# Moving k's and q's transfers up, delaying a piece's rounding by two half iterations, and letting conversion steps into lighter slots of a one-core attention and two-layer MLP kernel

## The chip, the cores and the metric

The kernel runs on one core of a Trainium2 chip. The metric is the device time of one execution in microseconds, as a median over runs. The engines are named as in the profile: PE is the matrix engine (PEld its weight load), DVE, ACT and POOL are the vector, scalar and GpSimd engines, and SP is the queue that issues the transfers.

## The reference

For 8 batches of 8 heads with 576 positions of 64 values, 32 packed queries `p` attend to `k`, `v`; then `q` attends to the 32 results. The attention output, laid out as 4608 tokens of 512 values, goes through two layers:

```python
h = x @ w_in;  g = max(h, 0) + alpha * min(h, 0);  x = g @ w_out          # d_ff 2048
g = x @ w_gate;  y = (silu(g) * (x @ w_val)) @ w_out2                     # d_ff 1536
```

[...] Every weight is widened on the chip from its two 32-bit words to a 32-bit float, and then split into a rounded high part and a low part, so that three matmuls (low by high, high by high, high by low) give the product.

## The kernel before

**Two stages.** The first stage has 256 iterations `it` of the first layer. `h_unit(it)` makes 128 hidden values of half a batch (288 tokens), and `o_unit(it - 3)` multiplies those of three iterations ago by `w_out` into four PSUM accumulators (`LAG1 = 3`). The hidden PSUM tiles, `g32` and `m` have two buffers each. 32 iterations belong to a batch. The second stage has 72 steps of the second layer, `gv_step`, fed from DRAM copies of its split weights (`wgvd`, `wo2d`).

**Half iterations.** `plan` holds side work for each half iteration, called a slot (`slot = 2 * it + late`), so a batch has 64 slots. While the 64 slots of one batch run, `attention(b)` makes the next batch's attention, for b = 2 to 7, by the table `STEPS`: a number is the slot's offset in the 64, the names behind it are the steps. `k0` to `k3` and `q0` to `q3` are loads of two heads each, four DMAs a load. `kt0` to `kt3` and `qt0` to `qt3` transpose them on DVE (L620). `s1a`, `s1b` are the first logits on PE and need all four kt. `mx`, `exp`, `sums` are their softmax, `et0`, `et1` transposes of it on PE, `pp0`, `pp1` products with v, whose results ACT scales into `ppbd` (L708), `ppt` a transpose of `ppbd`. `s2a`, `s2b`, `top`, `sub`, `sum`, `mul`, `turn`, `rest` are the second attention.

**Weight conversion.** From slot 84 on, each slot ends with `more_weights2`, which advances a generator over the 36 pieces of the second layer's weights. A piece is fetched by one DMA (L931), then `widen` makes an absolute value on ACT (L224), five DVE steps (L226, L230, L239, L248, L256) and a sum on POOL (L267). `split2` then rounds a half of it on ACT (L943), takes the difference on POOL (L944) and stores both (L945). For w_gate and w_val there are differences of quarters on POOL (L961) as well, which are split too. The generator yields a letter ahead of each step: `v` for a DVE step, `p` for POOL and for a `split2`, `a` for the absolute value. A slot grants at most two v, two p and one a; a slot in the set `busy` (a step on DVE that is not in `LIGHT`, a `PPW` slot, a `LEAVE` slot) grants no v. The absolute value waits until `LANDING` slots after the slot of the fetch.

**What orders instructions.** Matmuls are in program order (`behind`). On DVE and ACT a slot's steps stand behind the previous iteration's `m` (L1033) and `g` (L1036), and the rounding `hi` (L1044) of two iterations ago. A planner orders the rest by program order and by when it expects operands, buffers and engines to be free. SP and POOL are tied by that alone. Tiles of the tag `u` (k, q, their transposes, E, ET, s2, a) share 8 buffers, which are given out in program order, so a load cannot be placed ahead of the buffers that the program asks for before it. Each engine then runs its own list in order.

Of the kernel before, what the change touches and what calls it, by code (L numbers as in the profile page):

```python
# [71 lines left out]


STEPS = """
    8:p,k0,k1 10:pt 11:kt0,k2 12:kt1,k3,v0 14:kt2 15:kt3 17:s1a 19:s1b 20:mx0,q0,q1 21:mx1,exp0
    22:exp1 23:sums 24:et0 26:pp0,v1 27:et1 28:qt0,q2 29:qt1,q3 33:qt2 34:qt3 35:pp1 37:ppt 40:s2a
    42:s2b 44:top0 45:top1 46:sub0 47:sub1 49:sum0 50:sum1 51:mul0 52:mul1 53:turn0 54:turn1
    57:rest0 58:rest1
"""

LIGHT = {"p", "pt", "et0", "et1", "pp0", "pp1", "ppt", "s1a", "s1b", "exp1", "sums"}
PPW = (48, 55, 60, 66)

LEAVE = (6, 7, 38, 39)
# [3 lines left out]


GROUP0 = 84  # L90
LANDING = 5


FIRST_X = dict(load=-36, A11=-27, S=-26, S2=-25, A12=-12, D4=-11, S3=-11, S1=-10, A22=-8, S4=-7)
# [11 lines left out]
def f32(ap):  # L106
    return ap.bitcast(F32)
# [3 lines left out]
def tile_kernel(  # L111
# [93 lines left out]
    def like(ap, other):  # L205

        return ap if len(other.shape) == 2 else ap.rearrange("p (c f) -> p c f", c=KC)
# [8 lines left out]
    def widen(src, raw, val, out=None, n_piece=-1):  # L216

        if src is not None:
            issued.append(nc.sync.dma_start(out=like(raw, src), in_=src))
        words = raw.rearrange("p (n t) -> p n t", t=2)  # L220
        low, high = words[:, :, 0], words[:, :, 1]
        held = n_piece in HOLD
        with tc.issue_after(begun[HOLD[n_piece]].ins) if held else ExitStack():
            nc.scalar.activation(out=f32(val), in_=f32(high), func=AF.Abs)  # L224
        yield "v"
        nc.vector.tensor_scalar(  # L226
            out=f32(val), in0=f32(val), scalar1=E_TOP, scalar2=E_LOW, op0=ALU.min, op1=ALU.max
        )
        yield "v"
        nc.vector.tensor_scalar(  # L230
            out=val,
            in0=val,
            scalar1=3,
            scalar2=0x3FFFFFF8,
            op0=ALU.logical_shift_left,
            op1=ALU.bitwise_and,
        )
        yield "v"
        nc.vector.scalar_tensor_tensor(  # L239
            out=val,  # L240
            in0=high,
            scalar=0xC0000000,
            in1=val,
            op0=ALU.bitwise_and,
            op1=ALU.bitwise_or,
        )
        yield "v"
        nc.vector.tensor_scalar(  # L248
            out=high, in0=val, scalar1=0xFF800000, scalar2=None, op0=ALU.bitwise_and
        )  # L250
        yield "v"
        if n_piece in BY_POOL:
            nc.scalar.activation(out=f32(low), in_=low, func=AF.Copy, scale=2.0**-52)
            nc.gpsimd.tensor_tensor(out=f32(low), in0=f32(low), in1=f32(high), op=ALU.mult)
        else:
            nc.vector.scalar_tensor_tensor(  # L256
                out=f32(low),
                in0=low,
                scalar=2.0**-52,
                in1=f32(high),  # L260
                op0=ALU.mult,
                op1=ALU.mult,
            )
        yield "p"
        full = f32(val) if out is None else like(f32(val), out)
        other = f32(low) if out is None else like(f32(low), out)
        nc.gpsimd.tensor_tensor(  # L267
            out=full if out is None else out, in0=full, in1=other, op=ALU.add
        )
# [542 lines left out]
    for f in range(NF1):  # L812
# [8 lines left out]
        a=quad(0),  # L821
        b=quad(1, ["h"], evac=nc.vector),
        c=quad(2),
        d=quad(3, ["h", "at"]),
# [47 lines left out]
    def at(it, late, fn):  # L872

        plan.setdefault((it, late), []).append(fn)
# [7 lines left out]
                order += [(j, f, f == fs[0], f == fs[-1]) for f in fs]  # L882

    NB1 = 2 * NF1
    busy = set()
    for key, script in EARLY.items():
        at(*key, lambda script=script: run(script))

    for b in range(2, B):
        d0 = 2 * NB1 * (b - 1)  # L890
        steps_of = attention(b)
        for entry in STEPS.split():
            d, names = entry.split(":")
            slot = d0 + int(d)
            for n in names.split(","):
                at(*divmod(slot, 2), steps_of[n])
                if n[1:].isdigit() or n in LIGHT:
                    continue
                busy.add(slot)
        for j, d in enumerate(PPW):  # L900
            at(*divmod(d0 + d, 2), lambda b=b, j=j: pp_win(b, j))
            busy.add(d0 + d)
        busy.update(d0 + d for d in LEAVE)

# [3 lines left out]
    spots = {}  # L910

    def weights2():
        a, b = (t for t in raw_tiles)
        spots["raw"] = a[:, :1024]
        spots["g"], spots["v"] = a[:, 1024:1536], a[:, 1536:2048]
        spots["st"] = [b[:, i * 512 : (i + 1) * 512] for i in range(4)]
        spots["n"] = 0
# [9 lines left out]
    def fetch2():  # L927

        src = next(coming, None)
        if src is not None:  # L930
            nc.sync.dma_start(out=like(spots["raw"], src), in_=src)  # L931
            spots["landed"] = spots["slot"] + LANDING

    def piece2(name):
        yield "a"
        yield from widen(None, spots["raw"], spots[name])

    def split2(full, out):

        stage = spots["st"][spots["n"] % 4].bitcast(F32R)  # L940
        spots["n"] += 1
        hi, lo = stage[:, :256], stage[:, 256:]
        nc.scalar.activation(out=hi, in_=full, func=AF.Copy)  # L943
        nc.gpsimd.tensor_tensor(out=lo, in0=full, in1=f32(hi), op=ALU.subtract)  # L944
        nc.sync.dma_start(out=out, in_=f32(stage).rearrange("p (t n) -> p t n", t=2))  # L945

    def all_weights2():


        weights2()  # L950
        gv = {n: f32(spots[n]) for n in "gv"}
        b11, b21 = gv["g"][:, :256], gv["g"][:, 256:]
        b12, b22 = gv["v"][:, :256], gv["v"][:, 256:]
        fetch2()
        for f in range(NF2):

            def split(k, full):
                split2(full, wgvd[f][:, :, k, :])

            def less(out, x, y):  # L960
                nc.gpsimd.tensor_tensor(out=out, in0=x, in1=y, op=ALU.subtract)  # L961

            yield from piece2("g")
            yield "p"
            fetch2()
            split(0, b11)
            yield "p"
            split(2, b21)
            yield from piece2("v")
            yield "p"  # L970
            fetch2()
            split(6, b22)
            for out, x, y in (b11, b12, b11), (b12, b22, b12), (b22, b22, b11), (b21, b21, b22):
                yield "p"
                less(out, x, y)
            for k, full in (4, b11), (3, b12), (1, b22), (5, b21):
                yield "p"
                split(k, full)
            yield from piece2("g")
            for t in range(2):  # L980
                yield "p"
                if t == 0:
                    fetch2()
                c = slice(256 * t, 256 * t + 256)
                split2(gv["g"][:, c], wo2d[f][:, :, c])

    work2 = all_weights2()
    kinds = []

    def more_weights2(vector, slot):  # L990

        spots["slot"] = slot
        left = dict(v=2 if vector else 0, p=2, a=1)
        if not kinds:
            kinds.append(next(work2, None))
        while kinds[0] is not None and left[kinds[0]]:
            if kinds[0] == "a" and slot < spots["landed"]:
                return
            left[kinds[0]] -= 1
            kinds[:] = [next(work2, None)]  # L1000
# [318 lines left out]
    def steps(it, late):  # L1319


        with ExitStack() as held:
            if chained:
                for ins in made.get(it - 1), begun.get(it - 1), rounded.get(it - 2):
                    if ins is not None:
                        held.enter_context(tc.issue_after(ins.ins))
            for s in plan.get((it, late), ()):
                s()
            slot = 2 * it + late
            if slot >= GROUP0:  # L1330
                more_weights2(slot not in busy, slot)

    due = []
    for it in range(N1 + LAG1):
        if it == CHAIN0:
            chained.append(it)
        steps(it, 0)
        if it < N1:
            h_unit(it)
        steps(it, 1)  # L1340
        due.extend(range(max(it - LAG1, 0), it - LAG1 + 1))

        if it < N1 and len(due) == 1 and order[due[0]][2]:
            continue
        while due:
            o_unit(due.pop(0))
# [44 lines left out]
```

## Time and profile before

| | |
|---|---|
| median of 3 runs | 1673.23 us (1671.7 to 1676.21) |
| the profiled execution | 1670.67 us, its span 1668.9 us |
| PE busy | 1602.7 us, 96% of the span |
| DVE, ACT, POOL busy | 52%, 41%, 42% |
| mean granted clock of PE | 0.982 of full speed |

The span runs from the first to the last instruction of the profiled execution. A busy share is a sum over stages with different limits; PE's ends of matmuls are modelled.

### The profile page before, as it was taken

What the parts mean: (1) busy time and instruction counts of PE and PEld (TensorE: products, weight loads), DVE (VectorE), ACT (ScalarE), POOL (GpSimd) and SP (SyncE); (2) the same over time, 40 slices, a digit from 0 to 9 for tenths busy, and PEclk for the clock granted to TensorE, in tenths of its full rate; (3) what the DMA queues carried; (4) which work ended last, traced back from release to release, by engine and by line L of the source; (5) the groups of instructions that cost most, each with busy time, mean ns of one, the idle gap of its engine ahead of it and who ended that gap; (6) DMA issues with size and microseconds to landing.
All of it is one profiled execution on the core that took longest, in us unless ns stands there. A gap on an engine that the chain in (4) does not pass through costs nothing.

```text
span 1668.9 us, 28555 instructions
## 1 busy us (share of the span) xinstructions
PE 1602.7 (96%) x10708; PEld 1451.7 (87%) x10708; DVE 873.4 (52%) x1549; ACT 678.6 (41%) x1523; POOL 706.5 (42%) x764
## 2 busy tenths in 40 slices
PE   5798899999999999999999999999999999999997
PEld 3567698888898989889999999999999999999997
DVE  6989757575666667575334433442442443344222
ACT  5765655555565555555422222232232222223222
POOL 3556754565565555656223222322322322232222
PEclk7799999999999999999999999999999999999999
DMA  9433464635646363652654563464455456445342
GB/s 235 128 106 108 124 159 126 168 113 140 167 118 181 99 176 95 158 162 88 231 202 157 187 217 139 180 228 148 177 179 206 166 181 215 147 163 208 141 175 82
DMA packets 230443, 266.12 MB, mean 159 GB/s; under 512 B 130464, under 2 KB 196000, under 8 KB 230304
## 3 DMA queue, kind: packets, MB, share of 16 engines
q1 hardware_dynamic: 230304, 264.30, 50.5%
q8 instruction: 84, 1.38, 0.4%
q14 instruction: 55, 0.45, 0.1%
HBM read 214.70 MB, written 49.55 MB: 158 GB/s over the span
## 4 chain that ended last, share of the span: by engine, by line
PE 55%; issue 18%; POOL 9%; DVE 9%; DMA 5%; ACT 2%; SPq 2%; POOLq 0%; DVEq 0%; ACTq 0%
PE acc L1059 5%; PE acc L1060 4%; PE acc L1065 4%; PE o L308 4%; PE o L309 4%; PE o L307 4%; POOL pl L1278 3%; PE yb L307 3%; PE yb L309 3%; PE yb L308 3%; PE h L307 2%; PE h L309 2%; PE h L308 2%; PE xb L308 2%; PE vb L308 2%
## 5 line engine op out<-in xcount | busy, mean ns | idle before, releaser
L1046 POOL TENSOR_TENSOR lo<-g,hi 128x288 fp32r<-128x288 f32 x256 | 228.0, 892 | 242.6 <-ACT hi L1044 194.1
L1258 POOL TENSOR_TENSOR s<-s,u 128x384 f32<-128x384 f32 x72 | 73.1, 1015 | 490.5 <-ACT s L1252 490.5
L1036 DVE SCALAR_TENSOR_TENSOR g<-h,sg,m 128x288 f32<-128x288 f32 x256 | 130.2, 509 | 170.4 <-ACT m L1033 146.3
L1215 DVE TENSOR_TENSOR u<-yb,p 128x384 f32<-128x384 f32 x144 | 80.1, 556 | 255.2 <-PE yb L309 255.2
L1278 POOL TENSOR_TENSOR pl<-s,ph 128x384 fp32r<-128x384 f32 x144 | 145.4, 1031 | 106.5 <-ACT ph L1276 104.7
L1215 DVE TENSOR_TENSOR u<-vb,u 128x384 f32<-128x384 f32 x144 | 80.4, 558 | 197.7 <-PE vb L309 197.6
L1044 ACT ACTIVATE hi<-g 128x288 fp32r<-128x288 f32 x256 | 112.8, 441 | 151.7 <-DVE g L1036 149.5
L307 PE MATMUL h<-a2h,ppw 128*128 128x288 f32 x512 | 160.4, 313 | 13.1 <-DVE g L1036 7.7
L309 PE MATMUL o<-wp,ph 128*128 128x512 f32 x432 | 171.4, 397 | 0.0
L308 PE MATMUL o<-wp,ph 128*128 128x512 f32 x432 | 170.9, 396 | 0.0
L307 PE MATMUL o<-wp,pl 128*128 128x512 f32 x432 | 168.8, 391 | 0.9 <-POOL pl L1278 0.9
L1252 ACT ACTIVATE s<-p 128x384 f32<-128x384 f32 x72 | 37.9, 526 | 302.0 <-DVE p L1215 302.0
L309 PE MATMUL h<-a2l,ppw 128*128 128x288 f32 x512 | 152.3, 297 | 0.0
L308 PE MATMUL h<-a2h,ppw 128*128 128x288 f32 x512 | 151.9, 297 | 0.0
L1033 ACT ACTIVATE m<-h,sal 128x288 f32<-128x288 f32 x256 | 126.0, 493 | 51.7 <-PE h L309 50.7
L307 PE MATMUL yb<-ring,gv 128*128 128x384 f32 x432 | 145.9, 338 | 0.4 <-DVE u L1215 0.3
L309 PE MATMUL yb<-ring,gv 128*128 128x384 f32 x432 | 144.4, 334 | 0.0
L308 PE MATMUL yb<-ring,gv 128*128 128x384 f32 x432 | 144.4, 334 | 0.0
L307 PEld LDWEIGHTS h<-a2h,ppw 128*128 128x128 f32 x512 | 97.4, 190 | 44.7 <-DVE g L1036 14.5
L1276 ACT ACTIVATE ph<-s 128x384 fp32r<-128x384 f32 x144 | 69.8, 519 | 121.3 <-DVE s L1256 121.2
L309 PEld LDWEIGHTS h<-a2l,ppw 128*128 128x128 f32 x512 | 97.2, 190 | 0.8 <-issue 0.8
L308 PE MATMUL vb<-ring,gv 128*128 128x384 f32 x288 | 97.6, 339 | 0.0
(228 smaller groups left out, 4178.3 us busy)
## 6 DMA issues: line engine op xcount, KB each, us to landing
gv<-wgvd SPq DMA_DIRECT2D x144, 896.0 KB, 5.7
wgvd<-cva SPq DMA_DIRECT2D x84, 256.0 KB, 3.1
cva<-in_moe_w_out_dram SPq DMA_DIRECT2D x28, 512.0 KB, 4.1
v<-in_v_dram SPq DMA_DIRECT2D x16, 576.0 KB, 5.6
out_dram<-os SPq DMA_DIRECT2D x12, 768.0 KB, 3.8
cva<-in_moe_w_in_dram SPq DMA_DIRECT2D x16, 512.0 KB, 3.9
kr<-in_k_dram SPq DMA_DIRECT2D x96, 72.0 KB, 2.9
qr<-in_q_dram SPq DMA_DIRECT2D x96, 72.0 KB, 2.6
```

The lines of the kernel that those rows point to most:

```text
L307: nc.tensor.matmul(o, wlo, xhi, start=start, stop=False, **kw)
L308: nc.tensor.matmul(o, whi, xhi, start=False, stop=False, **kw)
L309: return nc.tensor.matmul(o, whi, xlo, start=False, stop=stop, **kw)
L1033: begun[it] = nc.scalar.activation(out=m, in_=hp, func=AF.Copy, scale=sal[:, f : f + 1])
L1036: made[it] = nc.vector.scalar_tensor_tensor(out=g32, in0=hp, scalar=sg[:, f : f + 1], in1=m, op0=ALU.mult, op1=ALU.max)
L1044: rounded[n] = nc.scalar.activation(out=hi, in_=x, func=AF.Copy)
L1046: nc.gpsimd.tensor_tensor(out=lo, in0=x, in1=f32(hi), op=ALU.subtract)
L1059: nc.tensor.matmul(acc[dc], lo[:, f % WP, c], ghi, start=start, stop=False)
L1215: return nc.vector.tensor_tensor(out=out, in0=bank, in1=x, op=ALU.add)
L1258: latest.append(nc.gpsimd.tensor_tensor(out=s2, in0=s2, in1=u3, op=ALU.mult))
L1276: nc.scalar.activation(out=hi, in_=x, func=AF.Copy)
L1278: nc.gpsimd.tensor_tensor(out=lo, in0=x, in1=f32(hi), op=ALU.subtract)
```

## The change

`STEPS` gives k0, k1 at offset 2 and k2, k3 at 3, ahead of all transposes of k (before: 8, 8, 11, 12, with k2 and k3 behind kt0 and kt1). q0, q1 go from 20 to 17, q2 from 28 to 25, q3 stays at 29; p goes from 8 to 5. After a piece's sum, the generator fetches the next source at once and yields `w`, which holds it until `SETTLE = 2` slots after the slot of the sum, so that the first rounding comes then. Roundings have a letter of their own, `s`, one a slot; POOL's differences keep `p`, two a slot. `LANDING` goes from 5 to 6. The slots of `HALF` and `LEAVE`, which granted no DVE step, grant one.

```diff
 STEPS = """
-    8:p,k0,k1 10:pt 11:kt0,k2 12:kt1,k3,v0 14:kt2 15:kt3 17:s1a 19:s1b 20:mx0,q0,q1 21:mx1,exp0
-    22:exp1 23:sums 24:et0 26:pp0,v1 27:et1 28:qt0,q2 29:qt1,q3 33:qt2 34:qt3 35:pp1 37:ppt 40:s2a
+    2:k0,k1 3:k2,k3 5:p 10:pt 11:kt0 12:kt1,v0 14:kt2 15:kt3 17:s1a,q0,q1 19:s1b 20:mx0 21:mx1,exp0
+    22:exp1 23:sums 24:et0 25:q2 26:pp0,v1 27:et1 28:qt0 29:qt1,q3 33:qt2 34:qt3 35:pp1 37:ppt 40:s2a
     42:s2b 44:top0 45:top1 46:sub0 47:sub1 49:sum0 50:sum1 51:mul0 52:mul1 53:turn0 54:turn1
     57:rest0 58:rest1
+HALF = {"mx0", "mx1", "top0", "top1", "sum0", "sum1"}
-LANDING = 5
+LANDING = 6
+SETTLE = 2
-    busy = set()
+    busy, partly = set(), set()
-                busy.add(slot)
+                (partly if n in HALF else busy).add(slot)
-        busy.update(d0 + d for d in LEAVE)
+        partly.update(d0 + d for d in LEAVE)
     def piece2(name):
         yield "a"
         yield from widen(None, spots["raw"], spots[name])
+        spots["summed"] = spots["slot"] + SETTLE
+        fetch2()
+        yield "w"
             yield from piece2("g")
-            yield "p"
-            fetch2()
+            yield "s"
             split(0, b11)
...
-        left = dict(v=2 if vector else 0, p=2, a=1)
+        left = dict(v=vector, p=2, s=1, a=1, w=99)
-            if kinds[0] == "a" and slot < spots["landed"]:
+            if slot < spots.get({"a": "landed", "w": "summed"}.get(kinds[0]), 0):
                 return
-                more_weights2(slot not in busy, slot)
+                more_weights2(0 if slot in busy else 1 if slot in partly else 2, slot)
```

## Rows read from the trace of the kernel before

**Rows 1.** Windows: stretch, its us, busy us per engine (instructions), clock, DMA.

```profile
280.00:380.00 100.00, 94.11 (x852) 84.36 (x851) 65.30 (x118) 53.03 (x126) 58.88 (x69) 1.00 0.52 138
380.00:472.00 92.00, 88.63 (x798) 81.43 (x791) 59.49 (x104) 48.50 (x117) 52.91 (x63) 0.98 0.51 133
472.00:562.00 90.00, 88.10 (x807) 80.06 (x807) 59.93 (x107) 50.28 (x120) 53.18 (x64) 1.00 0.53 141
562.00:654.00 92.00, 89.72 (x819) 81.66 (x818) 60.32 (x107) 50.35 (x120) 53.39 (x65) 1.00 0.53 140
654.00:746.00 92.00, 90.05 (x822) 81.99 (x821) 60.57 (x107) 50.09 (x120) 54.31 (x65) 1.00 0.54 149
820.00:1669.00 849.00, 839.72 (x4380) 777.56 (x4378) 309.67 (x548) 220.43 (x459) 232.87 (x228) 1.00 0.50 177
```

**Rows 2.** Waits of PE, 200 to 800 us: total us, times, longest.

```profile
PE et L684 <- ACT ppbd L708: 4.8, 4, 1.8
PE s L570 <- DVE kT L620: 4.6, 4, 1.8
PE h L307 <- DVE g L1036: 3.2, 4, 1.3
PE pp L700 <- ACT ET L691: 0.9, 2, 0.6
...
PE ppt L632 <- ACT ppbd L708: 0.8, 2, 0.5
```

**Rows 3.** Waits of PE's weight loads, 200 to 800 us.

```profile
PEld s L570 <- DVE kT L620: 7.2, 5, 2.3
PEld et L684 <- ACT ppbd L708: 5.8, 4, 2.0
```

**Rows 4.** Waits of ACT and DVE, 200 to 800 us.

```profile
ACT cva L943 <- POOL cva L267: 26.5, 27, 2.9
...
ACT cva L224 <- DMA cva<-in_moe_w_val_dram: 13.6, 8, 3.3
DVE kT L620 <- DMA kr<-in_k_dram: 13.1, 7, 3.1
...
ACT cva L224 <- POOL cva L944: 3.8, 4, 1.7
```

**Rows 5.** Timeline of SP's queue in one batch: start, us, line, transfer.

```profile
481.40 1.46 SPq L598 DMA_DIRECT2D kr<-in_k_dram  x2
...
538.17 5.69 SPq L598 DMA_DIRECT2D kr<-in_k_dram  x8
559.58 0.39 SPq L931 DMA_DIRECT2D cva<-in_moe_w_val_dram  x1
```

**Rows 6.** Timeline of all engines around one wait of et1, 508 to 510.6 us.

```profile
508.00 1.28 POOL L267 TENSOR_TENSOR cva<-cva 128x512 f32<-128x512 f32 x1 [1.15 <-PE pp L700]
...
509.31 0.72 ACT L943 ACTIVATE cva<-cva 128x256 fp32r<-128x256 f32 x2 [0.54 <-POOL cva L267]
...
509.94 0.29 ACT L708 ACTIVATE ppbd<-pp,sums 128x64 f32<-128x64 f32 x1
...
510.29 0.42 PE L684 MATMUL et<-ident,E 128*96 128x128 f32 x2 [1.47 <-ACT ppbd L708]
```

**Rows 7.** Single lines on DVE: duration ns min/median/max, 200 to 800 us.

```profile
L226 DVE TENSOR_SCALAR cva<-cva x36: 384/428/1078, 223.5 to 769.8; 128x512 f32<-128x512 f32 x36
...
L230 DVE TENSOR_SCALAR cva<-cva x36: 416/428/1036, 224.0 to 770.5; 128x512 uint32<-128x512 uint32 x36
...
L239 DVE SCALAR_TENSOR_TENSOR cva<-cva x36: 674/691/1315, 225.5 to 771.0; 128x512 uint32<-128x512 uint32 x36
```

**Rows 8.** Timeline of POOL and of DVE at one such step.

```profile
503.98 0.81 POOL L1046 TENSOR_TENSOR lo<-g,hi 128x288 fp32r<-128x288 f32 x1 [3.73 <-ACT hi L1044]
...
504.06 1.01 DVE L230 TENSOR_SCALAR cva<-cva 128x512 uint32<-128x512 uint32 x1
```

**Rows 9.** Windows, as rows 1: offsets 52 to 55 of one batch.

```profile
546.30:552.20 5.90, 5.90 (x53) 4.90 (x52) 4.69 (x9) 3.95 (x9) 2.97 (x3) 1.00 0.02 4
```

More of the change, by code (lines that the diff above doesn't have):

```diff
@@ L963, in all_weights2 @@
             yield from piece2("g")
-            yield "p"
-            fetch2()
+            yield "s"
             split(0, b11)
-            yield "p"
+            yield "s"
             split(2, b21)
             yield from piece2("v")
-            yield "p"
-            fetch2()
+            yield "s"
             split(6, b22)
@@ L976, in all_weights2 @@
             for k, full in (4, b11), (3, b12), (1, b22), (5, b21):
-                yield "p"
+                yield "s"
                 split(k, full)
@@ L980, in all_weights2 @@
             for t in range(2):
-                yield "p"
-                if t == 0:
-                    fetch2()
+                yield "s"
                 c = slice(256 * t, 256 * t + 256)
```

## The prediction

> **What bounds the kernel now.** I read the windows first, to see where PE stands still. In the second stage it is busy 839.7 of 849 us, and nothing of the change runs there; the stretch from 280 to 746 us, five batches long, leaves PE idle 5.89 + 3.37 + 1.90 + 2.28 + 1.95 = 15.4 us [rows 1]. DVE, ACT and POOL are each busy about two thirds of it or less, so no other engine is the bound over a batch: what can be won is PE's idle time and little else. Two batches before 280 us belong to the start, where other conversions run; I count nothing there.
>
> Next I read PE's waits from 200 to 800 us for the causes. The two largest are 4.8 us of et1 behind ACT's L708 and 4.6 us of the logits s1 behind the transposes kT; then 3.2 us of h behind g, 0.9 of pp behind ET and 0.8 of ppt behind L708 [rows 2]. Four of the five are what the change is about. The same waits as PE's weight loads see them are longer, 7.2 us for s1 and 5.8 for et [rows 3]: a matmul's end is modelled, and PE had run dry a little before it counts as idle. So the first view bounds each wait from below, the second from above.
>
> Then I followed both back. DVE waits 13.1 us in 7 places for k to land before it transposes [rows 4]. The timeline of SP shows why: k2's first transfers go at 481.4 us, when the transposes of that batch are already due, while the eight DMAs of the next batch's k0 and k1 go at 538.17, some 36 us ahead of theirs [rows 5]. k0 and k1 stand behind nothing but free buffers; k2 and k3 stand behind kT0 and kT1 in the order in which the shared buffers are given out. The et1 wait is a queue: POOL sums a piece from 508.00 for 1.28 us, ACT's two roundings L943 wait for it and run from 509.31 to 510.03 (0.54 us of ACT's wait shows), and only then comes L708 at 509.94, for which PE stood still until 510.29, 1.47 us [rows 6]. L943 waits 26.5 us for that sum in 27 places [rows 4].
>
> **The change part by part.**
>
> *k written together.* With k0 to k3 ahead of every kT, all sixteen DMAs can go where eight go now. The added eight cost SP as much as the eight there, 5.69 us [rows 5]. In the trace SP does nothing from 543.9 (538.17 + 5.69) until the next fetch at 559.58, whose sum is not ready before; that gap of 15.7 us hides them. If that cover went, the fetch would be up to 5.7 us late, some four slots of 90 / 64 = 1.4 us [rows 1], and the absolute value would wait on ACT as it already does in places (13.6 us in 8 places for w_val alone [rows 4]). k then lands more than 20 slots before kt0, so DVE's 13.1 us of waiting go and with it PE's wait of s1: 4.6 to 7.2 us [rows 2, 3]. The buffers allow it: at that point the live ones of the eight are s2 and a, four tiles, and k takes the other four; kT takes those of s2 and a, whose last readers stand at offset 58.
>
> *q and p.* q0 and q1 still stand behind E0 and E1, q2 comes three slots earlier, ahead of ET1. No wait of PE hangs on q, so I count 0; the cover is the distance from qt3 at 34 to s2a at 40. p moves past nothing on PE's path: 0.
>
> *Rounding two slots later.* Two slots are 2.8 us; the sum takes 1.28 and ACT's longest wait for it is 2.9 [rows 4, 6]. So the roundings find it done, and L708 no longer stands behind a blocked queue. Gone: et 4.8 to 5.8 us, ppt 0.8 us, and most of pp's 0.9 [rows 2, 3]. What is late next is on ACT: b21's rounding (the last of a pair of pieces) and the next piece's absolute value now share a slot, and the latter writes what POOL's L944 of the former still reads. Before, a slot lay between, and the wait was 3.8 us in 4 places at most 1.7 [rows 4]. There are 12 such places now. If each takes the longest that rows show, ACT loses 20 us in all. I cost that at 0 on PE, because `o_unit` runs three iterations behind `h_unit`, and ACT's waits of up to 3.3 us for a fetch [rows 4] cost PE no more than the 0.9 us of pp in the whole stretch. If the cover went, it is up to 1.7 us a place.
>
> *LANDING.* One slot more for the fetch can only shorten ACT's wait. The total length changes little: walking the generator slot by slot by the two rules, the last step comes at slot 463 instead of 461, at iteration 231, and its first reader in the second stage is later: 0.
>
> *DVE steps in lighter slots.* The same walk gives what moves into offsets 44 to 54, where the second attention already fills DVE: four steps in the first batch (L226, L230, L239, L248), three in the second (L239, L248, L256), one in the third (L226), two in each of the three after (L226, L230). That is 5 of L226, 4 of L230, 2 each of L239 and L248, one L256. I price L248 as L230, L256 as L239, their nearest forms. At the medians 5 x 0.43 + 4 x 0.43 + 2 x 0.69 + 2 x 0.43 + 0.69 = 6.8 us; at the longest 5 x 1.08 + 4 x 1.04 + 2 x 1.32 + 2 x 1.04 + 1.32 = 15.6 us [rows 7]. The two lengths are not noise: an L230 that begins at 504.06, while POOL is in an instruction until 504.79, takes 1.01 us instead of 0.43 [rows 8]. What hides them is DVE's free time: 5.90 - 4.69 = 1.2 us at offsets 52 to 55 with PE busy throughout [rows 9]. Two steps (0.9 us) fit; four (2.0) and three (1.8) overrun by 0.8 and 0.6. At the medians PE thus pays 1.4 us, at the longest up to the whole 15.6. POOL is busy 53.2 of 90 us [rows 1], so some steps will be long: I take 2.5.
>
> The Trainium skill has a rule on this that speaks against the change: SBUF — State Buffer, section "Who interferes with whom", says that VectorE and GpSimd share one pair of ports as an exclusive lock, and whichever comes second waits for the whole instruction. The trace agrees at the step just shown, 1.01 us beside 0.43. If every moved step met a POOL instruction, the rule would make the sum of this part 15.6 us, if none did, 6.8.
>
> *The sum.* Gain at least 4.6 + 4.8 + 0.8 + 0.9 = 11.1 us, at most 7.2 + 5.8 + 0.8 + 0.9 = 14.7; I take the middle, 12.9, since both views miss part of a stall's length. Less 2.5 is 10.4. From the profiled execution, 1670.67 - 10.4 = 1660.3. The median of the runs is 2.6 us above that execution, so 1662.8 for the runs.
>
> **The rivals.**
>
> *The queue refills.* The roundings give way, but the new wait of the absolute value behind L944, or a late fetch, blocks L708 in their place. For it: L708 stands in ACT's list behind whatever the planner thinks is ready first, and the new wait is in all 12 places. Against it: by the walk those places fall on offsets 10, 38 and the like, while pp0 is at 26. Then only k's part comes: 5.9 (the middle of 4.6 and 7.2) - 2.5 = 3.4 us, 1669.4: within 0.3%, which is 5 us and about what a measurement of this kernel can tell from no change.
>
> *DVE becomes the bound at offsets 44 to 54.* The moved steps delay g there, h waits for its buffer, and PE stands still once a batch. For it: the rule above, and a free 1.2 us only. Against it: g has over an iteration of slack, since h has two buffers, and the waits of h on g are 3.2 us in all. At the full 15.6 us the change costs 15.6 - 12.9 = 2.7 us, 1675.9; it is slower from the point at which PE pays over 12.9 us, that is about 2.1 in each of the six batches. To be slower by over 0.3% it must pay 17.9, which needs the delayed ppw or s2 steps to add to it.
>
> *More goes than is counted.* DVE freed from waiting for k also makes g earlier: the 3.2 us of h [rows 2] go too, the upper bound 14.7 holds and nothing new comes: 17.9 us, 1655.3.
>
> **How the numbers follow.** The forecast 0.68, its own range 1658 to 1667.5 (11.1 - 5 to 14.7 of gain). The queue refills 0.17, DVE bound 0.08 (half of it beyond 0.3%), more than counted 0.07. Faster by over 0.3% (under 1668.2): the forecast and the last, less a little for the forecast's edge, 0.72. Slower by over 0.3%: 0.06, with a little for what the planner may reorder. The same: 0.22. The range takes in the refilled queue and the last case: 1655 to 1672.
>
> **What would show it.** Right: no wait of s on kT and none of kT on kr; sixteen kr in one run on SP near offset 44; L943's wait for L267 a small part of 26.5 us; PE's idle time from 280 to 746 us down from 15.4 to about 3 to 5. Wrong: h waiting for g at offsets 46 to 56 (DVE bound); et or ppt still behind L708, with L224 before it (refilled queue); kr waiting on SP for a buffer; or a longer start before 280 us, where a planner that orders anew could move several us that I counted as unchanged.

## The result and the profile after

The changed kernel takes 1651.35 us (1648.82 to 1653.71, 4 runs), the kernel before 1672.91 beside it (1671.7 to 1676.21, 4 runs). The ratio is 0.9872, with a 95% interval from 0.9857 to 0.9887. It is faster by 21.6 us: the sign forecast, twice the 10.4 us forecast, and outside the range. The span of the profiled execution falls from 1668.9 to 1647.0 us, with the same mean granted clock, 0.982.

The first view is the windows again, over five batches, each from the `m` of iteration 64 to that of iteration 224. The first row is of before, the second of after; the columns are those of [rows 1].

```profile
284.30:746.40 462.10, 447.40 (x4065) 407.02 (x4050) 301.76 (x532) 251.44 (x601) 271.23 (x323) 1.00 0.53 142
```

```profile
280.80:723.90 443.10, 441.51 (x4071) 405.28 (x4070) 299.73 (x535) 255.25 (x602) 275.19 (x324) 1.00 0.55 147
```

Five batches are 19.0 us shorter, and the start ahead of them 3.5, all of it between iterations 32 and 64. What follows is as long as it was: 923.1 us to the end of the span, 922.5 before. PE's idle time falls from 14.7 to 1.6 us, which is 13.1 of the 19.0. The other 5.9 us are a fall of PE's busy time, for the same matmuls. Some 1.7 us of them are the clock, which the mean of 1.00 hides. In the trace of before, PE stood still for et1 and then ran at half the clock, the level of 1.2 GHz:

```profile
417.86 0.66 PE L684 MATMUL et<-ident,E 128*96 128x128 f32 x2 [1.75 <-ACT ppbd L708]
```

```profile
417.00:422.00 5.00, 4.14 (x20) 4.13 (x21) 1.86 (x3) 1.70 (x6) 1.98 (x3) 0.66 0.84 222
```

A clock of 0.66 over 5 us is 3.4 us at 0.50, which cost 1.7 us. (It is also the 0.98 in the second line of [rows 1].) The change has no such stretch after 280 us but for the last 6 us of the span, where PE comes to its end. The remaining 4.2 us are stalls that had been booked as busy time; that this comes from the modelled ends of matmuls is an inference. The weight loads agree with it: they stand idle 55.1 us in the row of before (462.10 - 407.02) and 37.8 in that of after (443.10 - 405.28), 17.3 less, and with 1.7 of clock that is the 19.0.

PE's waits from 200 to 800 us are these three, where [rows 2] had 4.8 us of et, 4.6 of s and 3.2 of h:

```profile
PE s L572 <- ACT ppT_3b L721: 1.2, 1, 1.2
PE h L309 <- DVE g L1038: 0.3, 1, 0.3
PE et L686 <- ACT ppbd L710: 0.3, 1, 0.3
```

ACT's waits in the same stretch, beside [rows 4] (lines have moved by 2 to 6: L226 was L224, L949 was L943, L950 was L944):

```profile
ACT cva L949 <- POOL cva L269: 18.4, 24, 2.1
...
ACT cva L226 <- DMA cva<-in_moe_w_gate_dram: 4.6, 4, 1.4
...
ACT cva L226 <- POOL cva L950: 4.4, 5, 1.7
```

Two things are to be seen. The rounding L949 still waits 18.4 us for POOL's sum, although it now comes two slots later. But the absolute value hardly waits for its transfer any more: 4.6 us for w_gate and 3.2 in 2 places for w_val, against 12.0 in 8 places and 13.6 [rows 4]. The new wait behind L950 is 4.4 us, as small as it was.

SP's queue at the place of the third row of [rows 5], start, us, line and transfer:

```profile
519.35 0.39 SPq L933 DMA_DIRECT2D cva<-in_moe_w_gate_dram  x1
520.61 2.49 SPq L951 DMA_DIRECT2D wo2d<-cva  x2
523.20 10.82 SPq L600 DMA_DIRECT2D kr<-in_k_dram  x15
540.45 0.39 SPq L933 DMA_DIRECT2D cva<-in_moe_w_val_dram  x1
540.88 0.58 SPq L600 DMA_DIRECT2D kr<-in_k_dram  x1
```

The transfers of k now go almost in one run between two fetches. No wait of DVE for k is left. The last row is of offsets about 47 to 52, where steps moved into lighter slots:

```profile
525.30:531.30 6.00, 6.00 (x47) 6.00 (x46) 5.97 (x12) 2.53 (x7) 2.67 (x3) 1.00 0.68 108
```

DVE is busy 5.97 of 6.00 us, and PE all 6.00. DVE is full here and costs PE nothing.

### The profile page after: what moved, and what is told of

It reads as the page before. It is cut to its first block, busy times and chain, and to the rows that moved or that the text cites. A ratio compares the mean times of both kernels' runs of the same rounds, so it can differ in the third digit from the quotient of the medians.

```text
span 1647.0 us, 28556 instructions
## 1 busy us (share of the span) xinstructions
PE 1596.5 (97%) x10708; PEld 1449.8 (88%) x10708; DVE 871.9 (53%) x1549; ACT 682.5 (41%) x1523; POOL 708.3 (43%) x764
## 4 chain that ended last, share of the span: by engine, by line
issue 39%; PE 36%; POOL 15%; DVE 6%; ACT 2%; DMA 1%; SPq 1%; POOLq 0%; ACTq 0%; DVEq 0%
POOL pl L1280 9%; PE acc L1061 7%; PE acc L1067 7%; PE acc L1062 7%; POOL s L1260 4%; PE h L309 4%; PE h L311 3%; PE h L310 3%; PE ppw L572 1%; DVE g L1038 1%; PE s L572 1%; DMA cva<-in_moe_w_in_dram 1%; POOL cva L269 1%; DVE cva L250 1%; SPq L358 1%
## 5 line engine op out<-in xcount | busy, mean ns | idle before, releaser
L1048 POOL TENSOR_TENSOR lo<-g,hi 128x288 fp32r<-128x288 f32 x256 | 228.1, 892 | 215.3 <-ACT hi L1046 173.8
L1254 ACT ACTIVATE s<-p 128x384 f32<-128x384 f32 x72 | 37.9, 526 | 302.0 <-DVE p L1217 302.0
```

The lines of the kernel that those rows point to most:

```text
L1048: nc.gpsimd.tensor_tensor(out=lo, in0=x, in1=f32(hi), op=ALU.subtract)
```

## The experiments

All times are medians in us beside runs of the kernel before on the same chip.

| kernel | time | before | ratio, 95% interval |
|---|---|---|---|
| A: before, new STEPS | 1660.79 | 1674.88 | 0.9914 (0.9891 to 0.9936) |
| B: before, roundings later | 1668.54 | 1674.88 | 0.9962 (0.9945 to 0.9979) |
| C: before, lighter slots | 1688.48 | 1674.88 | 1.0077 (1.006 to 1.0094) |
| D: after, no lighter slots, LANDING 5 | 1663.32 | 1674.88 | 0.9931 (0.9915 to 0.9947) |
| E: after, old STEPS | 1661.86 | 1672.52 | 0.9936 (0.9917 to 0.9955) |
| F: after, SETTLE 0 | 1651.86 | 1672.52 | 0.9874 (0.9853 to 0.9894) |
| G: after, LANDING 5 | 1671.0 | 1672.52 | 0.9993 (0.9978 to 1.0007) |
| H: before, lighter slots, LANDING 6 | 1662.63 | 1672.52 | 0.9945 (0.9926 to 0.9964) |
| I: before, LANDING 6 for 34 fetches | 1670.65 | 1672.0 | 0.9986 (0.9971 to 1.0001) |
| J: G, transfers halved | 1657.76 | 1672.0 | 0.9907 (0.9892 to 0.9922) |
| K: before, transfers halved | 1660.29 | 1672.0 | 0.9923 (0.9906 to 0.994) |
| L: after, lighter slots grant two | 1666.02 | 1672.0 | 0.9955 (0.994 to 0.997) |
| M: before, only k moved | 1658.56 | 1672.73 | 0.9919 (0.9903 to 0.9936) |
| N: before, only q moved | 1671.69 | 1672.73 | 0.9991 (0.9982 to 1.0001) |
| O: after without the later roundings | 1652.95 | 1672.73 | 0.9884 (0.9869 to 0.9899) |
| P: after, transfers halved | 1648.81 | 1670.43 | 0.9878 (0.9861 to 0.9895) |
| Q: after, LANDING 7 for 26 fetches | 1653.46 | 1670.43 | 0.9899 (0.9882 to 0.9916) |

**The parts alone.** A takes the table `STEPS` of the change and nothing else; B the fetch after the sum, `SETTLE` and the letter `s`, with LANDING 5; C the slots that grant one DVE step; D leaves these and the sixth slot out of the change.

> Only the table of attention steps is changed: k's transfers together at offsets 2 and 3, q's and p's earlier; conversion as before. Theory A (each wait has one cause, and costs more than PE's idle time shows, since short hold-ups are booked as busy): PE's waits of s on kT go, 7.8 us by the spacing of PE's matmuls, and the waits of et and ppt behind L708 stay: about 8 us faster, 1665. Rival B (k's transfers also stood ahead of the weights' fetches on SP, so that the absolute value came late on ACT and held up h): the waits of h go as well, 11 to 13 us faster, 1660 to 1662, and ACT's waits of L224 for a transfer fall from 25.6 to about 8 us. Rival C (DVE steps in lighter slots gave what the forecast lacked): 5 to 8 us, 1665 to 1668.

> Only the delayed rounding: the wait of two slots between sum and rounding, one rounding a slot, the fetch right after the sum; steps as before, no lighter slots, and the landing wait at 5 (at 6 the conversion would end too late without the lighter slots). Theory A: et, ppt and pp wait no more, 7.2 us by the spacing of the matmuls; s on kT stays: 7 us faster, 1666. Rival B: the same 7 us, with ACT's waits of L224 for a transfer about as long as before, 20 to 26 us. Rival C: 7 us or less. If the queue refills behind another ACT instruction: 0 to 3 us.

> Only the lighter slots: one DVE step in the slots of mx, top, sum and in the four left-out offsets; nothing else. Theory A and rival B: nothing is gained by it alone, PE's waits of s and et stay; the conversion ends some 50 slots earlier, so fetches come closer together: within 3 us of the time before, 1670 to 1676. Rival C (lighter slots spread DVE's work and take the waits of h on g away): 5 to 7 us faster, 1666 to 1668.

> The changed kernel without the lighter slots: no DVE step in them, and the landing wait back at 5, since the conversion would otherwise end too late. Theory A and rival B: as fast as the changed kernel but for the shorter landing wait, 1651 to 1656. Rival C: it loses the 5 to 7 us that the lighter slots gave, 1657 to 1659, with waits of h on g above 3 us.

A gains 14.1 us, far over the price of k. Its waits of et fall from 4.8 to 1.9 us, though it does nothing about roundings. ACT's waits for fetches fall from 25.6 (12.0 + 13.6) to 19.4 us. B gains 6.3, and its queue refills at another place: s2 waits for ACT's L721 in four batches, about 1 us each, a wait that the change itself has once. Ahead of L721 stand roundings that wait for their sum (0.5 us at 432.30) and for POOL's L967 (0.4 us at 433.12), not the absolute value or the fetch that the rival named. D, the table and the later roundings with five slots, gains 11.6, no more than the table alone; the same wait is 1.4 us in each of four batches there. C is slower by 13.6. Its waits of PE and ACT, 200 to 800 us:

```profile
PE h L308 <- DVE g L1037: 11.0, 10, 2.0
PE s L571 <- DVE kT L621: 5.2, 4, 3.1
```

```profile
ACT cva L944 <- POOL cva L268: 37.9, 34, 3.2
ACT cva L225 <- DMA cva<-in_moe_w_gate_dram: 16.9, 10, 3.3
ACT cva L225 <- DMA cva<-in_moe_w_val_dram: 14.6, 9, 3.7
```

h waits for g, as the rival of a full DVE has it. But ACT, whose `m` comes ahead of g, waits 31.5 us for fetches (16.9 + 14.6), where it waited 25.6, and 37.9 us for sums, where it waited 26.5; in the two longest of h's waits it had stood 3.2 us at L944 for a sum. That made the sixth slot, which I had priced at nothing, the suspect. A part of C's loss is the clock: in its profiled execution PE ran 17.1 us at half the clock between 280 us and the second stage, in four stretches, each at or right behind a wait of PE of 1.8 to 3.2 us. That is at most 8.5 us. Not every long wait has such a stretch: behind 1.79 us of s at 306.8 before has none.

**The sixth slot.** G and H each differ by that one constant from the change and from C. E and F each undo another part of the change.

```diff
-LANDING = 6
+LANDING = 5
```

> The changed kernel with the landing wait at 5 instead of 6: steps, delayed rounding and lighter slots stay. The runs so far: steps alone 14 us faster, the rounding alone 6, lighter slots alone 14 slower, steps and rounding without lighter slots 12 faster, all together 22. Theory L (what the last 10 us are is the sixth slot of waiting for the fetch, which the lighter slots only pay for: at 5, ACT stands 30 us or more at L224 for transfers, and h waits for g): loses most of it, 1658 to 1664, with ACT's wait at L224 for transfers back above 25 us. Rival C (the lighter slots themselves): 1651 to 1654.

> The kernel before with the lighter slots and the landing wait at 6, steps and rounding as before. Theory L: the 14 us that the lighter slots lost alone came from fetches that had not landed, and go: 1666 to 1674, with ACT's wait at L224 for transfers below 15 us instead of 31. Rival C' (the lighter slots cost DVE time at offsets 44 to 54, which the rest hides): still slower than before, 1678 to 1686, with waits of h on g of 8 us or more.

> The changed kernel with the old table of steps: k2 and k3 behind kT0 and kT1 again. Theory A (waits of s on kT alone): 8 us slower than the changed kernel, 1659, with 4 to 6 us of PE's wait of s on kT. Rival B (k's transfers also hold up the fetches and the stores on SP): 12 to 16 us slower, 1663 to 1667, with ACT's wait at L224 for transfers at 20 us or more.

> The changed kernel with SETTLE at 0: the first rounding may come in the slot of the sum. Theory A: L943's wait for the sum comes back in most pieces (18 us to 25 or more) and with it PE's waits of et and ppt behind L708: 5 to 7 us slower than the changed kernel, 1656 to 1659. Rival L: the rounding matters little beside the sixth landing slot: within 2 us, 1650 to 1654.

G loses the whole gain: 1671.0 against 1672.52 before. In H the sixth slot turns C's loss of 13.6 us into a gain of 9.9. H's largest wait of PE is s's:

```profile
PE s L571 <- DVE kT L621: 3.9, 5, 1.2
...
PE h L308 <- DVE g L1037: 0.9, 2, 0.6
```

h's 11.0 us are gone with the same slots open to DVE as in C, so a fuller DVE alone does not make C's loss. Whether it goes because fetches have landed or because the pieces fall on other slots, H does not tell, and no kernel with C's slots and halved transfers was run. G's waits are the counterpart:

```profile
PE h L309 <- DVE g L1038: 7.5, 5, 2.8
PE et L686 <- ACT ppbd L710: 3.0, 2, 2.4
```

```profile
ACT cva L226 <- DMA cva<-in_moe_w_gate_dram: 17.4, 9, 5.1
ACT cva L226 <- DMA cva<-in_moe_w_val_dram: 17.1, 8, 4.3
```

Two of G's 36 fetches stand on SP behind the change's own run of k, 2.9 and 2.5 us after the end of the sum that they wait for. The second of them, with the sum ahead of it and what follows:

```profile
643.59 1.31 POOL L269 TENSOR_TENSOR cva<-cva 128x512 f32<-128x512 f32 x1
```

```profile
637.95 9.36 SPq L600 DMA_DIRECT2D kr<-in_k_dram  x13
647.42 0.58 SPq L933 DMA_DIRECT2D cva<-in_moe_w_gate_dram  x1
```

```profile
652.65 0.67 ACT L226 ACTIVATE cva<-cva 128x512 f32<-128x512 f32 x1 [5.08 <-DMA cva<-in_moe_w_gate_dram]
```

```profile
656.48 0.61 PE L309 MATMUL h<-a2h,ppw 128*128 128x288 f32 x1 [2.81 <-DVE g L1038]
```

```profile
656.50:663.30 6.80, 5.81 (x23) 5.46 (x24) 5.10 (x9) 4.04 (x11) 4.24 (x5) 0.50 0.41 129
```

Four of G's five waits of h, 6.8 of the 7.5 us, follow these two fetches, and behind the longest come 6.8 us at half the clock, which cost at most 3.4. In the change no fetch goes more than 1.5 us after its sum. ACT's total of 34.5 us is not the price by itself: D has 34.6 us of these waits and gains 11.6.

E, without the new STEPS, keeps 10.7 us. F, without the two slots of settling, keeps everything, 20.7: its waits of et are 0.3 us, the same as in the change.

**Is it the transfer?** A sixth slot also moves every later step to other slots. J, K and P tell the two apart: they leave the slots alone and shorten the transfer.

```diff
-            nc.sync.dma_start(out=like(spots["raw"], src), in_=src)
+            dst = like(spots["raw"], src)
+            if "landed" in spots:
+                n = src.shape[1] // 2
+                dst, src = dst[:, :n], src[:, :n]
+            nc.sync.dma_start(out=dst, in_=src)
```

> The changed kernel with the landing wait at 5, and from the second fetch on only half of each source is transferred, so that the other half of a piece is converted from what the buffer held; every instruction and its place stay, only the transfers are shorter. Theory L: the transfers land about 1 us sooner, ACT's wait at L224 for them falls from 34.5 to below 20 us, and at least half of the 20 us that the landing wait of 5 cost come back: 1652 to 1661. Rival P (at 5 the pieces fall on worse slots, whatever the transfer): 1667 to 1672.

> The kernel before with the same halved transfers from the second fetch on (half of each piece is converted from what the buffer held). Theory L: 4 to 8 us faster, 1665 to 1669, ACT's wait at L224 for transfers from 25.6 to below 15. Rival P: within 3 us of before, 1670 to 1676.

> The changed kernel with half of each piece's transfer left out from the second fetch on (half of a piece is converted from what the buffer held), waiting six slots as the change does. The control for the two kernels with halved transfers and five slots, which gave back 12 and 13 us. If those gained because the fetch came too late for five slots, six slots leave 7.8 us of ACT's waits for fetches in all and PE waits of 1.8 us, so halving is worth 0 to 3 us: 1648 to 1652. If they gained because less traffic makes everything else faster, the same 12 to 13 us come here too: near 1639.

J gets 13.2 us of G's 20 back, with ACT's waits for fetches down from 34.5 to 18.5. Behind k's run two of its fetches still go 3.5 and 2.5 us after their sums, and 2.9 us of h follow them. K gains 11.7 on the kernel before, with waits of 14.8 instead of 25.6. P, the control with six slots, gains nothing beyond the change: 0.9878 against 0.9872. So it is not the lighter traffic that makes J and K faster, but that fetches came too late for five slots.

**What each part needs.** I gives the kernel before the sixth slot for 34 of its 36 fetches, without lighter slots; Q gives the change a seventh for 26; L lets the lighter slots grant two DVE steps.

> The kernel before with one change: the absolute value waits 6 slots instead of 5 after the fetch, for the first 34 of 36 pieces (for all of them the conversion would end too late without the lighter slots). Theory L (at 5 the transfer has often not landed; ACT then stands at L224, and the piece's DVE steps, its sum, L943, L708, hi and h come late one after the other): 6 to 10 us faster, 1663 to 1667, ACT's wait at L224 for transfers from 25.6 to below 10 us, and et's wait behind L708 shorter although the rounding is not delayed. Rival A (each wait has the cause that stood right before it): et and h stay, no change, 1670 to 1675.

> The changed kernel with a seventh slot for the first 26 fetches. If one more slot keeps paying, ACT's 7.8 us of waits for fetches go and the time falls by 2 to 5 us, to 1646 to 1649. If PE has no stall left that hangs on a fetch (1.8 us of waits in all from 200 to 800 us), it stays at 1650 to 1653. If the pieces that come later push the conversion's end into the last batch, as six slots did without the lighter slots, it is 1654 to 1658, with the lost time behind 700 us.

> The changed kernel with two DVE steps instead of one in the lighter slots, so DVE gets twice the added work at offsets 44 to 54. The rival of the prediction that DVE becomes the bound there: 3 to 10 us slower than the changed kernel, 1654 to 1661, with waits of h on g at offsets 46 to 56. If DVE's work there lies in h's slack: within 2 us, 1649 to 1653. The pieces also fall on other slots, so a difference that does not show as h waiting for g at these offsets speaks for neither.

I gains 1.4 us, and its interval includes no change. Its conversion ends later, which the single line L226 shows (first and last start); it ran from 223.5 to 769.8 before [rows 7]:

```profile
L226 DVE TENSOR_SCALAR cva<-cva x35: 383/427/1046, 224.7 to 790.2; 128x512 f32<-128x512 f32 x35
```

The batches from iteration 32 to 223 are 4.9 us shorter than before, but the last one is 5.4 longer, since conversion now runs beside the second stage's preparation. PE also ran 10.2 us at half the clock in I's profiled execution (at most 5.1 us), at or behind waits of s for kT of 3.2 and 2.0 us; no kernel with k moved has such waits. In the change the same line runs until 745.9: lighter slots pay for the sixth slot. Q is no faster than the change; its conversion runs to 786.8, and its last batch is 4.9 us longer than before's. L is slower than the change by some 14 us with 8.1 us of h behind g, but all except 0.3 us at h's offsets 0 to 8, not where the slots were filled, and its waits for fetches are up too (19.5 us). 2.4 us of the 8.1 follow a fetch that k's run holds for 2.4 us on SP. L does not tell a full DVE from pieces on other slots.

**Splitting STEPS, and the roundings beside the rest.** M moves only k, N only q; O has every part but the later roundings.

> The kernel before with k's transfers alone moved to offsets 2 and 3; q and p stay. Theory K (k's late landing is the root of more than s's wait: DVE stands at kT, the last step of the piece at offset 16 comes late, and with it the next fetch, the absolute value, its sum, L943, L708 and et1): most of the 14 us of the whole table, 10 to 14 us faster, 1658 to 1662, with et's wait behind L708 falling from 4.8 to about 2 us. Rival Q (q's earlier transfers, which leave SP before a fetch, give a part of their own): 6 to 8 us, 1664 to 1666, and et's wait as before.

> The kernel before with q's transfers alone moved (q0, q1 to 17, q2 to 25); k and p stay. Theory K: within 3 us of before, 1669 to 1675, PE's waits of s and et as before. Rival Q: 4 to 7 us faster, 1665 to 1668.

> The changed kernel without its rounding part: steps, lighter slots and landing wait of 6, with the roundings as before (right after the sum, two a slot, the fetch after the next grant). Theory K with L (et and ppt waited because the sum was late, and the sum because the transfers were): as fast as the changed kernel within 3 us, 1649 to 1655, et's wait under 1.5 us. Rival A (the delay of the rounding gave the 7 us of et, ppt and pp that were predicted): 1657 to 1660, with 4 us or more of et and ppt behind L708.

M gains 14.2 us, all that A did; N's interval includes no change. O gains 19.8, so the later roundings add some 2 us beside the rest by the medians, and F none; the intervals of O and of the change overlap.

## Why the prediction was wrong

The sign held, and most of what was to be looked for: no s waits for kT, SP shows k's run near offset 46, k's transfers wait 2.6 us in all on SP (3.8 before), and PE's idle time fell even below the 3 to 5 us foreseen. One of these did not hold: L949 still waits 18.4 us for its sum, not a small part of 26.5. The last rival, that more goes than is counted, came nearest with 17.9 us: h's 3.2 us fell to 0.3, as it says. And 3.5 of the 21.6 us lie ahead of 280 us, where nothing was counted. The sizes failed, in four steps.

**k written together: priced 4.6 to 7.2 us, measured 14.2 alone (M), and the whole table some 10.7 beside the rest (E's ratio against the change's).** I took PE's wait of s for all that a late k costs. The trace of before has more, at the place of [rows 6]; DVE, POOL, SP and ACT in order of time, with the idle time before each in brackets:

```profile
491.83 0.78 DVE L620 STREAM_TRANSPOSE kT<-kr 128x576 f32<-128x576 f32 x1 [0.87 <-DMA kr<-in_k_dram]
...
494.91 0.69 DVE L256 SCALAR_TENSOR_TENSOR cva<-cva 128x512 f32<-128x512 uint32 x1
```

```profile
496.22 1.31 POOL L267 TENSOR_TENSOR cva<-cva 128x512 f32<-128x512 f32 x1
```

```profile
498.33 0.44 SPq L931 DMA_DIRECT2D cva<-in_moe_w_gate_dram  x1
```

```profile
502.89 0.67 ACT L224 ACTIVATE cva<-cva 128x512 f32<-128x512 f32 x1 [2.25 <-DMA cva<-in_moe_w_gate_dram]
```

DVE stands at a transpose until k lands. The piece's five steps stand behind it, then the sum, and only then the next fetch goes, while the slot of its absolute value is fixed. 0.8 us more come from SP, where eight transfers of q stand behind k's scattered ones and in front of this fetch:

```profile
492.94 5.28 SPq L603 DMA_DIRECT2D qr<-in_q_dram  x8
```

So ACT stands 2.25 us for the transfer, with `hi`, `m` and all else queued behind it; the five DVE steps end late again, the next sum starts at 508.00, and L943, L708 and et1 follow as in [rows 6]. I had followed et1's wait back to that sum and stopped, one link short. In M, with k alone moved, the fetch goes 0.03 us after its sum and the same absolute value stands 0.57 us; in the change it stands for nothing:

```profile
489.92 0.66 ACT L224 ACTIVATE cva<-cva 128x512 f32<-128x512 f32 x1 [0.57 <-DMA cva<-in_moe_w_gate_dram]
```

```profile
487.10 0.65 ACT L226 ACTIVATE cva<-cva 128x512 f32<-128x512 f32 x1
```

Over the whole stretch, k's move alone takes et from 4.8 to 1.5 us and ACT's waits for fetches from 25.6 to 16.6.

**LANDING: priced 0.** The step read "can only shorten ACT's wait" and held that ACT's waits for a fetch "cost PE no more than the 0.9 us of pp in the whole stretch", because `o_unit` runs three iterations behind. But ACT's `m` is what g needs and h waits for, and L708 stands in the same queue. The sixth slot with the lighter slots is worth 9.9 us (H). In the change, taking it back costs 20 (G), of which halved transfers give 13.2 back (J, with P as the control). It is no separate gain: with five slots and without the lighter ones the change still gains 11.6 (D), and it is with the lighter slots that five are too few. The cover that was priced under k, the gap on SP that hides its run, held in the change and did not in G, where two fetches stood behind the run.

**Rounding two slots later: credited with et, ppt and pp, some 7 us; worth some 2 or none beside the rest (O, F).** "So the roundings find it done" did not come: L949 waits 18.4 us in 24 places for its sum with two slots of settling and 19.5 in 25 without (F). The waits of et, ppt and pp were at the end of the chain that begins with late transfers, and most of them go with it: without the later roundings, 1.2 us of et are left and none of ppt and pp (O). Alone, with five slots, the later rounding does gain 6.3 (B), so the queue was read rightly; its first cause was not. The queue refilled at L721 where five slots stayed (B, D), and not in the change.

**DVE steps in lighter slots: priced at a loss of 2.5 us; alone a loss of 13.6 (C), with the sixth slot part of a gain (H).** The mechanism priced, port conflicts that push DVE past its free time, cost PE next to nothing in the change, where h waits 0.3 us in all. (The walk also left out an L256 in the third batch, L258 at 431.02 in the trace after; it fits DVE's free time and changes no price. And the refilled queue's 1669.4 us should read 1669.9.) The conflict itself is there: in the trace after, an L232 that begins at 488.24 while POOL is in L1048 until 488.96 takes 1.01 us, as against 0.43 without. That agrees with the exclusive lock of the Trainium skill, SBUF — State Buffer, section "Who interferes with whom". What it costs depended on whether PE waited for g, and in the change it did not.

One step more was too narrow: "what can be won is PE's idle time and little else". 5.9 of the 19.0 us came out of PE's busy time, 1.7 of them by the clock. The two views bounded each wait, but not what its cause cost, since the same late transfers stood behind several waits and behind idle time that no row named: the weight loads' idle time fell by 17.3 us, against the 14.7 that were added up. With the parts measured in one order, k gives 14.2 us, sixth slot, lighter slots and q bring that to 19.8 (O), and the roundings to 21.6.

Open stay what besides the two fetches behind k's run makes up the part of G's loss that halved transfers don't give back, how C's loss divides between DVE's places and late transfers, what made L slow, and whether the later roundings give 2 us or none.

## What to carry to other kernels

Follow a wait on an in-order queue back until it reaches a transfer or an instruction that waits for nothing, before giving its cost to the last link; waits that share a root go together. Where a fetch is issued after the previous piece and its use stands in a fixed slot, the margin between them is a price of its own: vary that one constant, and halve the transfer as a control, before anything else is moved. See what stands on the queue in front of the fetch, too. Sum PE's waits as a lower bound, take PE's busy time per batch beside it, and read the granted clock in stretches of a few us: a mean of 1.00 over 462 us hid 3.4 us at half the clock.

## What was not expected of the hardware

PE's busy time holds stalls: the same five batches were booked at 447.4 us of matmuls before and 441.5 after, of which the clock explains 1.7 us. A stall can cost twice: behind 1.75 us without work in before, PE ran 3.4 us at half the clock, and behind 2.81 us in G 6.8. Fifteen transfers of k took SP 10.82 us to issue, 0.72 each, nearly eight slots. In the change they lie between two fetches, and no wait of PE follows them; in G thirteen of them held a fetch for 2.5 us.
